# Summed weight blocks by copies and adding transfers in DRAM, and accumulator marks taken into z2, in an attention-and-gMLP kernel

## The chip, the cores and the metric

The kernel runs on one core of a Trainium2 chip. The metric is device time in microseconds (us) of one execution. Five engines matter: TensorE (PE in the rows, with its weight loads as PEld), VectorE (DVE), ScalarE (ACT), GpSimd (POOL) and SyncE (SP). Transfers are started by SyncE (queue q1), GpSimd (q0) and ScalarE (q10), and are carried by sixteen DMA engines.

## The reference, cut to what matters

One input of 2048 tokens and 512 columns is normalised and goes through two branches: a local attention (32 heads of 16, eight taps two tokens apart) and a gMLP whose gate mixes all tokens with a matrix `w_sp` of 2048 x 2048.

```python
# xn = layernorm(x); F = 1792, Fh = 896
z  = gelu(xn @ w_in)                       # S x 1792
z1 = z[:, :Fh]; z2 = layernorm(z[:, Fh:])
g  = w_sp @ z2 + b_sp[:, None]             # 2048 x 2048 by 2048 x 896
b  = (z1 * g) @ w_out
s  = attention(xn @ wqkv) @ wo             # 8 taps, dilation 2, softmax
out = x + s * silu(b)
```

## The kernel before, in words

**Products.** Every fp32 matrix product is made of three matmuls over a high and a low part: high by high, high by low, low by high. The helper `split` makes the high part on ScalarE (L195) and the low part on VectorE (L197). A weight block of the program thus appears as `wsp_5r` (as loaded), `wsp_5h` and `wsp_5l`. The matmuls of the gate are at L825; a 128x512 product is what most of them do. Where `split` writes the operand that TensorE holds fixed, the rows call the target `BIG`.

**Stages, by TensorE's time.** An opening to 66 us; the three attention projections; z1 from 158 to 218 us (seven blocks of columns by four chunks of tokens, gelu at L709); z2 from 218 to 295 us; the gate to 574 us; then the output projections of the two branches, to 691 us. Attention itself (L573 to L646 on VectorE, L633 on GpSimd) has no place of its own: it has a low priority and fills VectorE and GpSimd from the projections to beyond 600 us. Its 32 score products are in the list `sums_of`, numbered in program order.

**z2.** A z2 row i holds two tiles of 128 tokens, i and 8 + i; there are eight rows. Each tile is made in two halves, 512 and 384 columns wide, with twelve matmuls each, and gelu at L733. VectorE takes the statistics (L742, L743) and adds epsilon to the variance (L745, operand `mvz`); GpSimd takes the power -1/2 and one product (L746, L748); two rows later ScalarE normalises (L754), `split` writes the result into `BIG`, and four subtractions and additions (L767) make the combinations that go to DRAM as `t_d`.

**The gate** is `w_sp @ z2` by a scheme of seven block products in place of eight, for two halves a = 0, 1 of the output rows: m1a, m1b, m2a, m2b, m6a, m6b, m7, m4, m5, m3. m1a starts at 295 us, m1b (its second half of accumulators) at 317, m6a at 386. Each product accumulates in the PSUM banks `banks[a, f]`, f = 0 to 3, which ScalarE fills first with the bias (`seed`, L843). A seed's values are added to only if a matmul has opened the bank. For half a = 1 the function `second_seeds`, the third step of m1a, does that by four matmuls of 512 columns (L984), whose result the seed overwrites; for a = 0 the z2 stage has opened them.

**Weight sums.** m6, m7, m5 and m3 take sums of blocks of `w_sp`. For each half a and each i of eight (sixteen rows in all), from t0, t1 (upper blocks) and l0, l1 (lower blocks):

```
s3 = l1 + t1    s1 = t0 + t1    s0 = t0 + s3    s2 = l0 + s0
```

The 128x512 sums go to DRAM (`sums_d`) and are loaded again as `ws_0r` and so on when a product wants them (`summed`). Six rows (a = 1, i = 0 to 5) are added on GpSimd in the opening and the projections. Eight rows (a = 0) are added on VectorE during z1 (`first_sums`, L393), loaded by SyncE's queue and stored by GpSimd's, in eight buffers (`t4`) that z1 and z2 results, `z1_d` loads and others share. The last two (a = 1, i = 6, 7) are added on VectorE in the buffers of loaded weights (`raw_sums`) during z2.

**What sets the order.** Each engine runs its instructions in one fixed order. A planner with its own model of durations makes it, from priorities and from the dependencies, the ones added by hand among them (`add_manual_dep`). A dependency called NOSYNC binds the order on one engine and makes no wait of its own; SYNC makes the instruction wait. One by hand puts attention product `sums_of[9]` behind the low part of the first weights: `first weights ahead`.

## Time and profile before

| | |
|---|---|
| median of 3 runs | 695.89 us (694.54 to 697.04) |
| profiled execution: its own time | 696.54 us |
| its span (first to last instruction) | 694.8 us |
| busy: TensorE, VectorE, ScalarE, GpSimd | 686.6, 619.4, 277.7, 215.2 us |
| share of 16 DMA engines: q1, q0, q10 | 43.6%, 20.9%, 11.7% |
| DRAM read, written | 122.4 MB, 59.3 MB |
| granted TensorE clock | 1.00 in all stages |

How to read the rows that come later. A row of the timeline gives start, duration, engine, line, operation, what it writes and reads, the shapes, and in brackets how long the engine had stood before it and what released it. Starts of TensorE's rows are the firm part; durations of matmuls overlap, so two starts are subtracted to get the cost of one. A row of groups gives the busy time and the mean in ns of one, and behind the next bar the idle time ahead of such instructions and what ended it. A row of windows gives the stretch, its length, and for PE, PEld, DVE, ACT, POOL and SP the busy time with the number of instructions, then the clock, the DMA share and GB/s. TensorE is busy nearly all the time, so an instruction of another engine matters when TensorE stands for it, and else not.

### The profile page before, as it was taken

What the parts mean: (1) busy time and instruction counts of PE and PEld (TensorE: products, weight loads), DVE (VectorE), ACT (ScalarE), POOL (GpSimd) and SP (SyncE); (2) the same over time, 40 slices, a digit from 0 to 9 for tenths busy, and PEclk for the clock granted to TensorE, in tenths of its full rate; (3) what the DMA queues carried; (4) which work ended last, traced back from release to release, by engine and by line L of the source; (5) the groups of instructions that cost most, each with busy time, mean ns of one, the idle gap of its engine ahead of it and who ended that gap; (6) DMA issues with size and microseconds to landing.
All of it is one profiled execution on the core that took longest, in us unless ns stands there. A gap on an engine that the chain in (4) does not pass through costs nothing.

```text
span 694.8 us, 9233 instructions
## 1 busy us (share of the span) xinstructions
PE 686.6 (99%) x3084; PEld 573.0 (82%) x3084; DVE 619.4 (89%) x866; ACT 277.7 (40%) x458; POOL 215.2 (31%) x242
## 2 busy tenths in 40 slices
PE   8999999999999999998999999999999999999998
PEld 7888888888888899986888888888888888888886
DVE  6776868999989989889999998999989999989775
ACT  4342234224424256865534544442334444211531
POOL 3104837372343322124123222223111201642320
PEclk9999999999999999999999999999999999999999
DMA  8769899969999865267899768667576692655796
GB/s 270 252 193 289 288 348 384 346 204 358 407 412 340 329 231 190 80 201 231 258 403 314 284 211 298 208 232 248 183 261 206 215 342 89 221 173 190 246 330 235
DMA packets 102223, 182.36 MB, mean 262 GB/s; under 512 B 9184, under 2 KB 45280, under 8 KB 102176
## 3 DMA queue, kind: packets, MB, share of 16 engines
q1 hardware_dynamic: 56624, 102.21, 43.6%
q0 software_dynamic: 13824, 52.24, 20.9%
q10 hardware_dynamic: 31728, 27.33, 11.7%
q8 instruction: 24, 0.39, 0.2%
q14 instruction: 23, 0.19, 0.1%
HBM read 122.42 MB, written 59.32 MB: 262 GB/s over the span
## 4 chain that ended last, share of the span: by engine, by line
PE 67%; DVE 13%; DMA 12%; ACT 3%; issue 3%; POOL 1%; SPq 1%; DVEq 0%; POOLq 0%; ACTq 0%
PE g L825 35%; PE b L1067 4%; PE b L1069 4%; PE b L1068 4%; PE qkv L387 4%; PE qkv L386 4%; PE qkv L385 4%; DMA sb<-in_w_sp 3%; PE s L1069 2%; PE s L1068 2%; PE s L1067 2%; DMA sums_d<-sb 2%; DVE zst L742 2%; DMA z_d<-z1t 1%; DVE xT L280 1%
## 5 line engine op out<-in xcount | busy, mean ns | idle before, releaser
L633 POOL TENSOR_TENSOR pv<-pv 128x1024 f32<-128x1024 f32 x29 | 69.6, 2399 | 96.2 <-DVE pv L620 85.9
L573 DVE TENSOR_TENSOR pr<-k,q 128x2048 f32<-128x2048 f32 x32 | 73.6, 2299 | 2.0 <-DMA k<-qkv_d 1.9
L620 DVE TENSOR_TENSOR pv<-v,lg 128x2048 f32<-128x2048 f32 x32 | 74.6, 2331 | 0.7
L580 DVE TENSOR_REDUCE lg<-pr 128x128 f32<-128x2048 f32 x32 | 73.0, 2281 | 0.1
L647 POOL DMA_DIRECT2D o_d<-tt x32 | 18.0, 562 | 138.9 <-DVE tt L646 103.8
L433 ACT ACTIVATE stage<-qkv 128x512 f32<-128x512 f32 x40 | 23.0, 590 | 30.8 <-DMA qkv_d<-stage 17.0
L807 POOL DMA_DIRECT2D ol<-o_d x32 | 17.7, 555 | 37.7 <-DVE BIG L197 11.1
L1078 ACT ACTIVATE bt<-b 128x512 f32<-128x512 f32 x16 | 9.4, 599 | 43.5 <-PE b L1069 39.4
L709 ACT ACTIVATE z1t<-z 128x512 f32<-128x512 f32 x28 | 15.5, 597 | 26.1 <-DMA z_d<-z1t 15.3
L280 DVE TENSOR_TENSOR xT<-xT,mr 128x512 f32<-128x512 f32 x20 | 14.9, 743 | 11.9 <-DMA mr<-mv_d 6.4
L732 PE MATMUL z<-w_0h,BIG 128*128 128x512 f32 x64 | 25.0, 391 | 0.0
L731 PE MATMUL z<-w_0l,BIG 128*128 128x512 f32 x64 | 25.0, 391 | 0.0
L730 PE MATMUL z<-w_0h,BIG 128*128 128x512 f32 x64 | 24.9, 390 | 0.0
L742 DVE BATCH_NORM_STATS2 zst<-zt 128x6 f32<-128x448 f32 x32 | 19.3, 613 | 6.1 <-ACT zt L733 6.0
L754 ACT ACTIVATE zt<-zt,nmz,mvz 128x896 f32<-128x896 f32 x16 | 17.5, 1129 | 18.0 <-POOL nmz L748 18.0
L638 DVE TENSOR_TENSOR pv<-pv 128x512 f32<-128x512 f32 x32 | 22.9, 716 | 0.0
L733 ACT ACTIVATE zt<-z 128x512 f32<-128x512 f32 (+1 forms) x32 | 15.9, 536 | 15.2 <-DMA sums_d<-sa 14.0
L732 PE MATMUL z<-w_1h,BIG 128*128 128x384 f32 x64 | 21.5, 336 | 0.0
L730 PE MATMUL z<-w_1h,BIG 128*128 128x384 f32 x64 | 21.5, 335 | 0.0
L731 PE MATMUL z<-w_1l,BIG 128*128 128x384 f32 x64 | 21.4, 335 | 0.0
L393 POOL TENSOR_TENSOR sb<-sa,sb 128x512 f32<-128x512 f32 x12 | 19.7, 1644 | 5.4 <-DMA sb<-in_w_sp 5.1
L195 ACT ACTIVATE BIG<-zl 128x512 fp32r<-128x512 f32 x20 | 12.5, 630 | 21.6 <-DVE zl L895 19.8
(478 smaller groups left out, 2296.2 us busy)
## 6 DMA issues: line engine op xcount, KB each, us to landing
qkv_d<-stage ACTq DMA_DIRECT2D x24, 512.0 KB
v<-qkv_d POOLq DMA_DIRECT2D x14, 704.0 KB, 5.4
k<-qkv_d POOLq DMA_DIRECT2D x13, 704.0 KB, 6.8
sums_d<-sa POOLq DMA_DIRECT2D x14, 512.0 KB, 7.8
sums_d<-sb POOLq DMA_DIRECT2D x14, 512.0 KB, 8.0
z_d<-z1t ACTq DMA_DIRECT2D x14, 512.0 KB
zl<-z_d SPq DMA_DIRECT2D x12, 512.0 KB
tr<-t_d SPq DMA_DIRECT2D x12, 384.0 KB
```

Of the source, the lines that this page charges most:

```text
L573: line(nc.vector.tensor_tensor(pr, taps(ks[u], j0), qb.unsqueeze(1).to_broadcast([P, W, NJ * CS]), op=ALU.mult))
L580: line(nc.vector.tensor_reduce(lgs[u][:, j0 * HS : (j0 + NJ) * HS].rearrange("p i w -> p w i"), pr.rearrange("p w (i d) -> p w i d", d=DH) ...
L620: line(nc.vector.tensor_tensor(pv.rearrange("p w (i d) -> p w i d", d=DH), taps(vs[u], j0).rearrange("p w (i d) -> p w i d", d=DH), lgs[u] ...
L633: eng.tensor_tensor(pv[:, 0:4], pv[:, 0:4], pv[:, 4:8], op=ALU.add)
L730: nc.tensor.matmul(pz, xh[:, k], wh, start=k == 0, stop=False)
L731: nc.tensor.matmul(pz, xh[:, k], wl, start=False, stop=False)
L732: nc.tensor.matmul(pz, xl[:, k], wh, start=False, stop=k == KB - 1)
L742: nc.vector.bn_stats(st[:, h], zt[:, h * FQ : (h + 1) * FQ])
L825: nc.tensor.matmul(pg, z[a], w[b], start=start and i == 0, stop=stop and i == 2, skip_group_check=seeded)
L1067: nc.tensor.matmul(pp[:, cols], hi, wh, start=k == 0, stop=False)
L1068: nc.tensor.matmul(pp[:, cols], hi, wl, start=False, stop=False)
L1069: nc.tensor.matmul(pp[:, cols], lo, wh, start=False, stop=k == n - 1)
```

## The change

**Sums.** Ten of the sixteen rows (all eight of a = 0 and i = 6, 7 of a = 1) are no longer added by VectorE. They are taken in five pairs of neighbouring rows (`THEIRS`). For each pair ScalarE's queue copies l1, t0, t0 and l0 from `w_sp` to four DRAM tensors `sums_q` (twenty copies, 16 x 8192 elements each), and GpSimd's queue adds t1, s3, t1 and s0 onto them by transfers that accumulate at the destination (twenty, 256 x 512 each). They come in five rounds, in which a sum is used only a round after it was made. `go_on` paces them: fourteen operations in z1 (at every second gelu), sixteen in z2 (at the gelu of each narrow half), ten in the products m1b, m2a and m2b. A copy is paced by order (NOSYNC), an adding transfer waits for the ScalarE instruction that it is tied to (SYNC). The six rows on GpSimd stay.

**Marks.** The four matmuls of `second_seeds` go. In z2 rows 6 and 7 the first matmul of each narrow half is 512 wide in place of 384 (the first 128 columns repeat columns of the wide half), covers the whole bank, and so opens the banks that the second half's seeds are put in. The narrow halves' results now lie in the last 384 columns of the bank.

**A product waits.** The dependency of `sums_of[9]` goes; `sums_of[12]` is put behind the epsilon step of the last z2 row (L774 of the new file, L745 of the old).

```diff
+MINE = HT - 2
+THEIRS = [(0, q) for q in range(HT // 2)] + [(1, q) for q in range(MINE // 2, HT // 2)]
...
-    sums_d = dram.tile([2, 2, HT, P, 2, CT], F32, name="sums_d")
+    sums_d = dram.tile([2, MINE, P, 2, CT], F32, name="sums_d")
+    sums_q = {
+        (a, n, q): dram.tile([2, P, CT], F32, name=f"sums_{a}_{n}_{q}")
+        for a, q in THEIRS
+        for n in range(4)
+    }
...
-    def added(ts, eng):
-        t0, t1, l0, l1 = ts
-        for out_, p_, q_ in ((l1, t1, l1), (t1, t0, t1), (t0, t0, l1), (l0, t0, l0)):
-            eng.tensor_tensor(out_, p_, q_, op=ALU.add)
-
-    def block_sums(a, i, tile_=None, eng=nc.vector, loads=nc.sync, stores=nc.scalar, behind=None):
-        top, low = [(tile_ or t4)(f"s{n}_{a}_{i}") for n in "ab"]
-        for t, r in ((top, 0), (low, HT)):
-            ins = loads.dma_start(t, w_sp[2 * a : 2 * a + 2, r + i].rearrange("c p t -> p c t"))
-            if behind:
-                tc.add_manual_dep(ins.ins, behind[0].ins.name, behind[1], reason="sums later")
-        added([top[:, 0], top[:, 1], low[:, 0], low[:, 1]], eng)
-        for r, t in enumerate((top, low)):
-            stores.dma_start(sums_d[a, r, i], t)
-
-    def raw_sums(a, i):
-        ts = [
-            fetch(w_sp[2 * a + c, r + i], CT, f"sr_{a}_{i}_{c}_{r}") for r in (0, HT) for c in range(2)
-        ]
-        added(ts, nc.vector)
-        for n, t in enumerate(ts):
-            nc.sync.dma_start(sums_d[a, n // 2, i, :, n % 2], t)
...
-    z1_sums = [(0, i) for i in range(HT)]
+    def pool_sums(i, *behind):
+        top, low = [early_tile(f"s{n}_{i}") for n in "ab"]
+        for t, r in ((top, 0), (low, HT)):
+            ins = nc.gpsimd.dma_start(t, w_sp[2:4, r + i].rearrange("c p t -> p c t"))
+            tc.add_manual_dep(ins.ins, behind[0].ins.name, behind[1], reason="sums later")
+        t0, t1, l0, l1 = [top[:, 0], top[:, 1], low[:, 0], low[:, 1]]
+        for out_, p_, q_ in ((l1, t1, l1), (t1, t0, t1), (t0, t0, l1), (l0, t0, l0)):
+            nc.gpsimd.tensor_tensor(out_, p_, q_, op=ALU.add)
+        for r, t in enumerate((top, low)):
+            nc.gpsimd.dma_start(sums_d[r, i], t)
+
+    def rows_of_2k(blocks_):
+        return blocks_.rearrange("s p t -> (s p t)").rearrange("(r x) -> r x", x=4 * CT)
+
+    def raw_blocks(a, n, q):
+        r, c = divmod(n, 2)
+        j = r * HT + 2 * q
+        return w_sp[2 * a + c, j : j + 2]
+
+    def copied(to, a, q, src):
+        return nc.scalar.dma_start(rows_of_2k(sums_q[a, to, q]), rows_of_2k(src(a, q))), NOSYNC
+
+    def plus(to, a, q, src):
+        ins = nc.gpsimd.dma_start(
+            rows_of_2k(sums_q[a, to, q]), rows_of_2k(src(a, q)), accum_op=ALU.add, max_dma_last_dim=2048
+        )
+        return ins, SYNC
+
+    def weight_sums():
+        t0, t1, l0, l1 = [lambda a, q, n=n: raw_blocks(a, n, q) for n in range(4)]
+        s0, s3 = [lambda a, q, n=n: sums_q[a, n, q] for n in (0, 3)]
+        rounds = (
+            ((copied, 3, l1),),
+            ((copied, 0, t0), (plus, 3, t1)),
+            ((plus, 0, s3), (copied, 1, t0)),
+            ((plus, 1, t1), (copied, 2, l0)),
+            ((plus, 2, s0),),
+        )
+        for ops in rounds:
+            for a, q in THEIRS:
+                for fn, to, src in ops:
+                    yield fn, to, a, q, src
+
+    coming_sums = weight_sums()
+
+    def go_on(n, behind):
+        for fn, *args in itertools.islice(coming_sums, n):
+            ins, how = fn(*args)
+            tc.add_manual_dep(ins.ins, behind.ins.name, how, reason="sums paced")
...
-    def first_sums(a, i):
-        block_sums(a, i, stores=nc.gpsimd)
-
-    first_sums(*z1_sums[0])
-
     for f in range(FB):
         pair_ = side_pair("w1_last") if f == FB - 1 else None
         wh, wl = prep(w_in1[:, f, :], KB * P, f"w1_{f}", pair_=pair_)
@@ -706,31 +730,36 @@
             if c % 2 == 0:
                 zp = t4(f"z1t_{f}_{c}")
             zt = zp[:, c % 2]
-            nc.scalar.activation(zt, pz, AF.Gelu_apprx_tanh)
+            out_of = nc.scalar.activation(zt, pz, AF.Gelu_apprx_tanh)
             if c % 2:
+                go_on(1, out_of)
                 nc.scalar.dma_start(z1_d[f, c - 1 : c + 1].rearrange("c p t -> p c t"), zp)
-        if f == 2:
-            first_sums(*z1_sums[FB])
-        if f < FB - 1:
-            first_sums(*z1_sums[f + 1])
...
-        (k, h): prep(w_in2[:, k, HALF[h]], WID[h], f"w2_{k}_{h}")
+        (k, h): prep(
+            w_in2[:, k, slice(FH - CT, FH) if (k, h) == (0, 1) else HALF[h]],
+            CT if (k, h) == (0, 1) else WID[h],
+            f"w2_{k}_{h}",
+        )
         for h in range(2)
         for k in range(KB)
     }
 
     def z2_half(j, h, zt):
         xh, xl = xn_at(j)
-        pz = mm(f"z2_{j}_{h}")[:, : WID[h]]
+        bank = mm(f"z2_{j}_{h}")
+        pz = bank[:, CT - WID[h] :]
         for k in range(KB):
-            wh, wl = [w[:, : WID[h]] for w in w2[k, h]]
-            nc.tensor.matmul(pz, xh[:, k], wh, start=k == 0, stop=False)
+            wh, wl = [w[:, CT - WID[h] :] if k == 0 else w[:, : WID[h]] for w in w2[k, h]]
+            if k == 0 and j % HT >= HT - 2:
+                nc.tensor.matmul(bank, xh[:, k], w2[k, h][0], start=True, stop=False)
+            else:
+                nc.tensor.matmul(pz, xh[:, k], wh, start=k == 0, stop=False)
             nc.tensor.matmul(pz, xh[:, k], wl, start=False, stop=False)
             nc.tensor.matmul(pz, xl[:, k], wh, start=False, stop=k == KB - 1)
-        nc.scalar.activation(zt[:, HALF[h]], pz, AF.Gelu_apprx_tanh)
+        return nc.scalar.activation(zt[:, HALF[h]], pz, AF.Gelu_apprx_tanh)
...
-        nc.vector.tensor_scalar(rstd, rstd, EPS, None, op0=ALU.add)
+        known = nc.vector.tensor_scalar(rstd, rstd, EPS, None, op0=ALU.add)
+        if i == HT - 1:
+            tc.add_manual_dep(sums_of[12].ins, known.ins.name, NOSYNC, reason="gate rows ahead")
...
-        if i in (1, 3):
-            raw_sums(1, HT - 2 + i // 2)
         if i < HT:
             raw_z[i] = [t4(f"zt_{j}").rearrange("p i t -> p (i t)")[:, :FH] for j in (i, HT + i)]
             for h in range(2):
                 for j, zt in zip((i, HT + i), raw_z[i]):
-                    z2_half(j, h, zt)
+                    out_of = z2_half(j, h, zt)
+                    if h:
+                        go_on(1, out_of)
...
+            if name != "m1a":
+                go_on(1, highs[-1])
...
-            pair_ = spatial.get((2 * a + c, js)) or spatial_block(2 * a + c, js)
-            if (a, c, js) == (0, 0, 6):
-                tc.add_manual_dep(
-                    sums_of[9].ins, lows[-1].ins.name, NOSYNC, reason="first weights ahead"
-                )
-            return pair_
+            return spatial.get((2 * a + c, js)) or spatial_block(2 * a + c, js)
...
-        return lambda s: prep(sums_d[a, half_, s, :, i], CT, f"ws_{a}{half_}{i}_{s}")
+        def w(s):
+            if a and s < MINE:
+                src = sums_d[half_, s, :, i]
+            else:
+                src = sums_q[a, 2 * half_ + i, s // 2][s % 2]
+            return prep(src, CT, f"ws_{a}{half_}{i}_{s}")
+
+        return w
...
     def second_seeds():
-        for f in range(ODD + 1):
-
-            nc.tensor.matmul(
-                banks[1, f], z2_block(0, f)[0], half(0), start=True, stop=True
-            )
         for f in range(ODD + 1):
             seed(1, f, biases[1][0])
```

Lines of the new file are higher by some 30: `split` is at L202 and L204, the seeds at L874, the epsilon step at L774, the attention pair at L649 and L609, the gate products at L930, the copies at L420.

ScalarE's order at the seeds, first before, then with the change (`wsp_nh` are weights of m1a and, from 0 again, of m1b; `g_0` to `g_3` are the seeded banks; `zt` the last z2 row):

```order
L195 ACTIVATE wsp_1h<-wsp_1r 128x512
L195 ACTIVATE wsp_2h<-wsp_2r 128x512
L195 ACTIVATE wsp_3h<-wsp_3r 128x512
L195 ACTIVATE wsp_4h<-wsp_4r 128x512
L195 ACTIVATE wsp_5h<-wsp_5r 128x512
L843 ACTIVATE g_0_3191<-b_bh 128x512
L843 ACTIVATE g_1_3192<-b_bh 128x512
L843 ACTIVATE g_2_3195<-b_bh 128x512
L843 ACTIVATE g_3_3196<-b_bh 128x512
L754 ACTIVATE zt_3059<-zt_3059,nmz,mvz 128x896
```

```order
L202 ACTIVATE wsp_0h<-wsp_0r 128x512
L202 ACTIVATE wsp_1h<-wsp_1r 128x512
L420 DMA sums_2_2_92<-in_w_sp 16x8192
L874 ACTIVATE g_0_3129<-b_bh 128x512
L874 ACTIVATE g_1_3130<-b_bh 128x512
L874 ACTIVATE g_2_3133<-b_bh 128x512
L874 ACTIVATE g_3_3134<-b_bh 128x512
L785 ACTIVATE zt_2995<-zt_2995,nmz,mvz 128x896
L785 ACTIVATE zt_2996<-zt_2996,nmz,mvz 128x896
L202 ACTIVATE wsp_2h<-wsp_2r 128x512
```

The seeds stood behind the high parts of wsp_1 to wsp_5; they stand behind wsp_1 now, with a copy ahead of them.

VectorE's order around the last z2 row's epsilon step (`mvz` of L745, now L774), first before, then with the change:

```order
L197 TENSOR_TENSOR wsp_0l<-wsp_0r,wsp_0h 128x512
L197 TENSOR_TENSOR wsp_1l<-wsp_1r,wsp_1h 128x512
L1006 TENSOR_TENSOR b_bl<-b_bh,b_bl 128x512
L573 TENSOR_TENSOR pr_4_1457<-k_0_1440,q_0_1441 128x2048
L638 TENSOR_TENSOR pv_4_1452<-pv_4_1452 128x512
L767 TENSOR_TENSOR zt_2975<-zt_2975 128x384
L743 BN_AGGR mvz<-zst_3153 128x2
L197 TENSOR_TENSOR wsp_2l<-wsp_2r,wsp_2h 128x512
L197 TENSOR_TENSOR wsp_3l<-wsp_3r,wsp_3h 128x512
L639 TENSOR_TENSOR pv_4_1452<-pv_4_1452 128x4x2x32
L767 TENSOR_TENSOR zt_2975<-zt_2975,zt_2976 128x384
L745 TENSOR_SCALAR mvz<-mvz 128x2
```

```order
L204 TENSOR_TENSOR BIG<-zt_2909,BIG 128x4x128
L204 TENSOR_TENSOR wsp_7l<-wsp_7r,wsp_7h 128x512
L771 BN_STATS zst_3091<-zt_2996 128x6
L798 TENSOR_TENSOR zt_2909<-zt_2909 128x384
L204 TENSOR_TENSOR BIG<-zt_2910,BIG 128x7x128
L772 BN_AGGR mvz<-zst_3091 128x2
L204 TENSOR_TENSOR wsp_0l<-wsp_0r,wsp_0h 128x512
L798 TENSOR_TENSOR zt_2909<-zt_2909,zt_2910 128x384
L204 TENSOR_TENSOR wsp_1l<-wsp_1r,wsp_1h 128x512
L774 TENSOR_SCALAR mvz<-mvz 128x2
L649 TENSOR_TENSOR pv_0_1531<-v_0_1525,lg_1464 128x2048
L609 TENSOR_REDUCE lg_1505<-pr_4_1518 128x8x16
```

The epsilon step stood behind the splits of wsp_0 to wsp_3 and two attention steps. With the change no attention step is left between the split of wsp_6 and it, and the product of 2048 columns (`pv`, L649) follows it.

VectorE's order at the start of m6a (`ws` are its summed weights, `zl` the gate products that wait for m2b's accumulators, `tr` the loaded combinations), first before, then with the change:

```order
L895 TENSOR_TENSOR zl_0_3829<-g_0_3191,zl_0_3829 128x512
L614 TENSOR_TENSOR lg_1485<-lg_1485,sm_1547 128x256
L197 TENSOR_TENSOR BIG<-tr_2_3907,BIG 128x2x3x128
L197 TENSOR_TENSOR ws_4l<-ws_4r,ws_4h 128x512
L620 TENSOR_TENSOR pv_0_1551<-v_1_1545,lg_1485 128x2048
L580 TENSOR_REDUCE lg_1525<-pr_4_1538 128x8x16
L895 TENSOR_TENSOR zl_0_3829<-g_1_3192,zl_0_3829 128x512
L895 TENSOR_TENSOR zl_2_3836<-g_2_3195,zl_2_3836 128x512
L197 TENSOR_TENSOR ws_5l<-ws_5r,ws_5h 128x512
L895 TENSOR_TENSOR zl_2_3836<-g_3_3196,zl_2_3836 128x512
L197 TENSOR_TENSOR BIG<-tr_4_3944,BIG 128x2x3x128
L197 TENSOR_TENSOR ws_6l<-ws_6r,ws_6h 128x512
```

```order
L930 TENSOR_TENSOR zl_2_3780<-g_3_3134,zl_2_3780 128x512
L204 TENSOR_TENSOR ws_2l<-ws_2r,ws_2h 128x512
L675 STREAM_TRANSPOSE tt_0_1631<-pv_0_1612 128x256
L204 TENSOR_TENSOR ws_3l<-ws_3r,ws_3h 128x512
L204 TENSOR_TENSOR BIG<-tr_0_3817,BIG 128x2x3x128
L649 TENSOR_TENSOR pv_4_1634<-v_0_1606,lg_1545 128x2048
L609 TENSOR_REDUCE lg_1626<-pr_0_1627 128x8x16
L204 TENSOR_TENSOR BIG<-tr_2_3851,BIG 128x2x3x128
L204 TENSOR_TENSOR ws_4l<-ws_4r,ws_4h 128x512
L204 TENSOR_TENSOR ws_5l<-ws_5r,ws_5h 128x512
L204 TENSOR_TENSOR ws_6l<-ws_6r,ws_6h 128x512
```

Before, the split of ws_4 and an attention pair (L620, L580) stood ahead of the last three gate products. Now all four are ahead of the splits of ws_2 to ws_4, and the attention pair stands between ws_3 and ws_4.

6 lines of the change are left out of this document (2 added, 4 removed).

## The prediction

> **What bounds the kernel now.** I read the page first (busy time and the chain), then TensorE's waits, then the timeline around the longest of them.
>
> ```profile
> span 694.8 us, 9233 instructions
> PE 686.6 (99%) x3084; PEld 573.0 (82%) x3084; DVE 619.4 (89%) x866; ACT 277.7 (40%) x458; POOL 215.2 (31%) x242
> PE 67%; DVE 13%; DMA 12%; ACT 3%; issue 3%; POOL 1%; SPq 1%; DVEq 0%; POOLq 0%; ACTq 0%
> ```
>
> TensorE is busy 99% of the span, but the chain runs over VectorE and DMA for a quarter of it: a busy TensorE was kept company by a second chain about as long. The waits say how often that second chain won.
>
> ```profile
> PE g L825 <- ACT g L843: 1.9, 1, 1.9
> PE g L825 <- ACT BIG L195: 0.2, 1, 0.2
> ```
>
> Everything else that TensorE waited for lies in the opening or is 0.2 us. So the change can act on TensorE's own work and on these two waits, and on nothing else but waits that it makes. The timeline prices them:
>
> ```profile
> 311.26 0.39 PE L825 MATMUL g<-wsp_5h,BIG 128*128 128x512 f32 x1
> 311.49 1.07 PE L984 MATMUL g<-BIG 128*128 128x512 f32 x4
> 312.39 0.39 PE L825 MATMUL g<-wsp_6h,BIG 128*128 128x512 f32 x1
> ...
> 314.89 0.39 PE L825 MATMUL g<-wsp_6h,BIG 128*128 128x512 f32 x1
> 317.17 0.50 PE L825 MATMUL g<-wsp_0h,BIG 128*128 128x512 f32 x1 [1.90 <-ACT g L843]
> 317.51 0.40 PE L825 MATMUL g<-wsp_0l,BIG 128*128 128x512 f32 x1
> ...
> 323.88 0.39 PE L825 MATMUL g<-wsp_3h,BIG 128*128 128x512 f32 x1
> 324.48 0.50 PE L825 MATMUL g<-wsp_7h,BIG 128*128 128x512 f32 x1 [0.21 <-ACT BIG L195]
> 324.81 0.39 PE L825 MATMUL g<-wsp_7l,BIG 128*128 128x512 f32 x1
> ```
>
> Durations overlap, so I count from start to start: a 512-wide matmul costs 0.227 us (311.26 to 311.49). The four marking matmuls cost 312.39 - 311.49 = 0.90. The first wait costs 2.28 instead of 0.23, and the matmul behind it 0.34: 2.16 lost. The second costs 0.60 and 0.33: 0.47 lost. All that there is to gain is 0.90 + 2.16 + 0.47 = 3.5 us, 0.5% of the span.
>
> **Why TensorE waited there.** The rows of the other engines, ScalarE first, then VectorE:
>
> ```profile
> 236.39 0.98 ACT L733 ACTIVATE zt<-z 128x512 f32<-128x512 f32 x2 [13.09 <-DMA sums_d<-sa]
> ...
> 313.99 0.64 ACT L195 ACTIVATE wsp_3h<-wsp_3r 128x512 fp32r<-128x512 f32 x1 [5.03 <-DMA wsp_3r<-in_w_sp]
> 315.37 0.63 ACT L195 ACTIVATE wsp_4h<-wsp_4r 128x512 fp32r<-128x512 f32 x1 [0.75 <-PE g L825]
> 316.53 2.14 ACT L843 ACTIVATE g<-b_bh 128x512 f32<-128x512 f32 x4
> ```
>
> ```profile
> 304.04 2.29 DVE L620 TENSOR_TENSOR pv<-v,lg 128x2048 f32<-128x2048 f32 x1
> 306.24 2.28 DVE L580 TENSOR_REDUCE lg<-pr 128x128 f32<-128x2048 f32 x1
> ...
> 318.58 0.16 DVE L745 TENSOR_SCALAR mvz<-mvz 128x2 f32<-128x2 f32 x1
> ```
>
> The four seeds of the second half (L843) stand on ScalarE behind weight copies that waited for a load, and for TensorE itself. Behind that is lateness from further back: the first z2 row's gelu stood 13.09 us for a buffer whose stores of summed weights had not landed, and at 304 VectorE put 4.4 us of attention ahead of the last z2 row, whose statistics were done only at 318.58.
>
> **The change, part by part.**
>
> *Marks and widening.* The marks go: -0.90. Four opening matmuls grow from 384 to 512 columns:
>
> ```profile
> L730 PE MATMUL z<-w_0h,BIG 128*128 128x512 f32 x64 | 24.9, 390 | 0.0
> L730 PE MATMUL z<-w_1h,BIG 128*128 128x384 f32 x64 | 21.5, 335 | 0.0
> ```
>
> 4 x (390 - 335) ns = +0.22. Both lie on TensorE with nothing beside them: -0.68, the sure part.
>
> *The first wait.* With no mark to wait for, the seeds need a free bank and the bias, and the new order has them behind wsp_1h and ahead of wsp_2h, so neither the load of 313.99 nor TensorE stands before them. They can run at about 309 to 311, and TensorE comes to them at about 314.4. Bounds 0 and -2.16; I take all of it, since both things that ended last there are behind the seeds now.
>
> *The gate on the last row (sums_of[12]).* The new VectorE order has, between the split of wsp_6 (done 304.04, by the start of the next row) and the row's mvz, ten operations: four of 512 (0.60 each by the m6 rows below), one of 896 (1.0), two of 384 (0.46), and the statistics (0.7): 5.0 us, so mvz at 309.1 instead of 318.58. GpSimd's power and products come next:
>
> ```profile
> 318.82 1.68 POOL L746 TENSOR_TENSOR mvz<-mvz,nhalf 128x2 f32<-128x2 f32 x1 [1.83 <-DVE mvz L745]
> 320.60 1.50 POOL L748 TENSOR_SCALAR nmz<-mvz 128x1 f32<-128x1 f32 x2
> ```
>
> GpSimd takes 1.8 to 3.2 us for these, ScalarE 2.1 for the two normalisations, 1.0 for wsp_2h and wsp_3h, 0.5 for the copy into BIG: row 7 arrives at 314.5 to 315.9. The new order wants it two matmuls into the second half, at 314.9: a wait of 0 to 1.0, in place of 0.47. Bounds -0.47 and +0.5; I take -0.2, because the lateness behind 304 shrinks too (next). Queued behind the gate on VectorE are the attention steps from pv(12) on; GpSimd's folds and the o_d stores wait for them, TensorE does not before 650 us, and it shows no wait there now.
>
> *The sums leave VectorE.*
>
> ```profile
> L393 DVE TENSOR_TENSOR sb<-sa,sb 128x512 f32<-128x512 f32 x16 | 11.3, 714 | 2.2 <-DMA sb<-in_w_sp 2.1
> L393 DVE TENSOR_TENSOR sa<-sa 128x512 f32<-128x512 f32 x8 | 5.4, 682 | 0.1
> L393 DVE TENSOR_TENSOR sa<-sa,sb 128x512 f32<-128x512 f32 x8 | 5.4, 681 | 0.1
> ```
>
> These 32 adds (22.1 us) and eight on raw tiles go, and with them the buffers that the 13.09 us stood on. Attention fills the time; TensorE waits for neither, so by itself I cost this at nothing. What it buys is z2 rows on time, the cover for the last two terms.
>
> *The transfers.*
>
> ```profile
> q1 hardware_dynamic: 56624, 102.21, 43.6%
> q0 software_dynamic: 13824, 52.24, 20.9%
> sums_d<-sb POOLq DMA_DIRECT2D x14, 512.0 KB, 8.0
> ```
>
> By these rows 512 KB (0.524 MB) take 0.524/52.24 x 20.9% x 694.8 = 1.46 us of all sixteen engines on GpSimd's queue and 1.55 on SP's; I use 1.5. Removed are 40 such transfers' worth (ten rows, four each): 60 us. Added are 20 copies (30 us) and 20 adds. No adding transfer is in the trace: one pass each is the lower bound (30 us), three (source, old value, result) the upper (90 us). I take two, 60 us: nearer the plain store than the upper end, since the old value is the only extra read. Net +30 us of engine time, spread thus:
>
> ```profile
> 158.00:228.00 70.00, 70.00 (x316) 58.69 (x315) 67.30 (x85) 25.81 (x42) 26.55 (x32) 1.00 1.01 381
> 228.00:262.00 34.00, 34.00 (x168) 30.11 (x167) 30.63 (x55) 15.33 (x26) 7.68 (x12) 1.00 0.69 263
> 262.00:306.00 44.00, 44.00 (x217) 39.15 (x216) 37.31 (x77) 32.55 (x52) 8.83 (x15) 1.00 0.47 154
> 328.00:392.00 64.00, 64.00 (x284) 52.99 (x283) 62.50 (x84) 28.05 (x47) 16.55 (x17) 1.00 0.89 313
> ```
>
> (The last three columns are clock, DMA share and GB/s.) The removed 60 us lie in the first two rows, so the full stretch to 228 empties; about six adds and four copies come into 262 to 306, which is half idle. Seven adds and three copies come into 328 to 392, where 7 us are free: that is the risk, priced as a rival. Issuing is covered: 20 copies at about 0.4 us on ScalarE, less than half busy up to 262, and 20 adds on GpSimd, where 16 stores of about the same price go. An add also waits for a ScalarE result and for the round before it; queued behind it on GpSimd are folds, attention loads and the z2 powers. The rounds are tens of us apart against 8.0 to land, so I cost that at nothing.
>
> The Trainium skill, "DMA: Bandwidth & Descriptors", section "Issuing engines are not separate DMA queues", says that transfers started by any engine run on the same sixteen engines; its section "Rules for kernel authors" says that an accumulating transfer reads its destination and writes it later. The share of 1.01 with three queues in use agrees with the first; no run here shows the second yet. They speak for the third rival.
>
> *The start of m6a.* In the new order VectorE splits ws_2 to ws_7 behind the last of the four gate products that wait for m2b's end (before, ws_4 was still ahead of three of them).
>
> ```profile
> 385.81 0.39 PE L825 MATMUL g<-ws_0h,BIG 128*128 128x512 f32 x1
> ```
>
> ```profile
> 385.85 0.68 DVE L197 TENSOR_TENSOR ws_4l<-ws_4r,ws_4h 128x512 fp32r<-128x512 f32 x1
> 386.45 2.28 DVE L620 TENSOR_TENSOR pv<-v,lg 128x2048 f32<-128x2048 f32 x1
> 388.66 2.28 DVE L580 TENSOR_REDUCE lg<-pr 128x128 f32<-128x2048 f32 x1
> 390.85 1.28 DVE L895 TENSOR_TENSOR zl<-g,zl 128x512 f32<-128x512 f32 x2
> ```
>
> Counted from m6a's first matmul, the last product can start at about 0.3. Then come product, ws_2, transpose, ws_3, an operand of 768 columns, an attention pair, another operand and ws_4: 5 x 0.6 less one still to come, 0.36, 2 x 0.87, 2 x 2.2, and ws_4's own 0.67, so 9.2 to 9.3. TensorE wants it after 39 matmuls, at 8.84: a wait of about 0.5. If VectorE is as late as in the rows above, where products that could start near 386.1 started at 390.85, it is 0.5 + 4.7 = 5.2. I take 0.5: with the gate at 309.1, the shapes of the rows up to there add up to 377.5, before the bank is done, so VectorE should wait for TensorE there.
>
> **The sum**, on the profiled execution's 696.54: -0.68 - 2.16 - 0.2 + 0.5 = -2.5, so 694.0. That execution lies 0.65 above the median of the runs shown (695.89); against the median the same sum gives **693.3 us**, 0.37% faster.
>
> **Rivals.**
> 1. *The waits move, they do not go* (row 7 or m6a takes about 2 us): -0.68 and little else, 695.2. For it: 62.5 of 64 us of VectorE are busy in 328 to 392, so any slip is passed on. Against: 27 us of its work are gone. 0.32.
> 2. *VectorE is late at m6a as before*: 695.89 - 0.68 - 2.36 + 5.2 = 698.1, slower. It decides from a lateness of about 2.6 us on, where 0.5 + 2.6 eats the 3.0 gained. 0.10.
> 3. *The adds fill the engines in 328 to 392.* At two passes, 7 x 3.0 + 3 x 1.5 = 25.5 us against 7 free; 18 us too much. Attention's transfers can give way, weight loads cannot for long; if a third reaches TensorE, 693.3 + 6 = about 699; at three passes 36 against 7, and past 702. At one pass it is nothing. 0.12.
>
> My forecast has 0.46. About 0.3% (2.1 us, near the spread of the runs shown) is what can be told from no change: faster is the forecast (0.46), same the first rival (0.32), slower the other two (0.22). The range runs from 692.2 (all 3.5 gained, less the widening, and a little noise) to 698.5 (takes in rivals 1 and 2 and the near edge of 3); the forecast's own is 692.3 to 693.8.
>
> **What would show it.** Right: no PE wait on the seeds (L874 now), ScalarE's first z2 gelu without a wait for sums, mvz of the last row before 311, a wait of under 1 us at m6a's ws_4l, and a share below 1 in 158 to 228. Wrong: a PE wait of over 1.5 us on BIG or ws_4l; a share above 0.95 in 328 to 392 with waits for wsp loads; adds landing in over 16 us; or folds on GpSimd waiting behind an add.

## The result, and the profile after

| | before | with the change |
|---|---|---|
| median | 695.38 us (694.54 to 697.04, 4 runs) | 740.04 us (738.02 to 741.58, 4 runs) |
| ratio | | 1.0637, 95% interval 1.0598 to 1.0677 |
| profiled execution, own time and span | 696.54, 694.8 us | 741.58, 739.8 us |
| mean granted TensorE clock | 1.000 | 0.972 |

The change makes the kernel 6.4% slower; the forecast was 0.37% faster (693.3 us, range 692.2 to 698.5). First the page of the changed kernel, its span and busy times:

```profile
span 739.8 us, 9132 instructions
PE 697.3 (94%) x3080; PEld 579.6 (78%) x3080; DVE 600.9 (81%) x826; ACT 283.5 (38%) x462; POOL 226.0 (31%) x246
```

The span grew by 45.0 us. TensorE has four matmuls fewer and is busy 10.7 us longer, at a granted clock below 1. Its waits (engine, line, what it waited for, total, times, longest), of which before had 1.9 and 0.2 us:

```profile
PE g L856 <- DVE wsp_12l L204: 13.5, 1, 13.5
PE g L856 <- ACT wsp_1h L202: 5.6, 1, 5.6
PE z L760 <- DVE lg L627: 4.7, 1, 4.7
PE g L856 <- ACT BIG L202: 4.5, 1, 4.5
PE g L856 <- ACT g L874: 2.8, 1, 2.8
PE g L856 <- DVE ws_4l L204: 2.6, 1, 2.6
```

TensorE's timeline at the longest one (start, duration, row), and the window around it, whose third number from the end is the clock:

```profile
400.00 0.39 PE L856 MATMUL g<-wsp_12h,BIG 128*128 128x512 f32 x1
413.86 0.79 PE L856 MATMUL g<-wsp_12l,BIG 128*128 128x512 f32 x1 [13.46 <-DVE wsp_12l L204]
414.45 0.63 PE L856 MATMUL g<-wsp_12h,BIG 128*128 128x512 f32 x1
414.87 0.63 PE L856 MATMUL g<-wsp_13h,BIG 128*128 128x512 f32 x1
415.30 0.63 PE L856 MATMUL g<-wsp_13l,BIG 128*128 128x512 f32 x1
...
392.00:425.00 33.00, 19.54 (x79) 15.62 (x78) 14.31 (x22) 4.11 (x8) 11.64 (x12) 0.79 0.78 206
```

Two costs stand here. One is the wait. The other comes behind it: from start to start the matmuls now take 0.42 to 0.43 us in place of 0.227, for some 4 us. Counted over the whole trace from 30 us on, the steps from start to start that are over 0.6 us too long are too long by 38.9 us together (nine of them; before, one of 2.1), and 55 steps that are less too long, by 10.4 us (before 1.1). Nearly all of the 55 lie in stretches where the trace's clock records stand at 0.50. Together that is 46.1 us more than before, against 45.0 us of span and 0.7 us of matmul work that the change takes away. So the loss is waits, and a slow clock behind the long ones. The Trainium skill, "TensorE: Matmul & The Clock Gate", section "Part 1: The HAM clock gate (the "warmup" mystery)", says that the array runs at half its clock until it has been busy for some 3.4 us; the trace agrees with half the clock and some 4 us of it, and the forecast had no such term.

Why VectorE brought wsp_12l so late. VectorE's timeline, then GpSimd's over the same time:

```profile
388.80 2.28 DVE L602 TENSOR_TENSOR pr<-k,q 128x2048 f32<-128x2048 f32 x1
410.38 0.69 DVE L667 TENSOR_TENSOR pv<-pv 128x512 f32<-128x512 f32 x1 [19.30 <-POOL pv L662]
...
413.12 0.68 DVE L204 TENSOR_TENSOR wsp_12l<-wsp_12r,wsp_12h 128x512 fp32r<-128x512 f32 x1
```

```profile
376.12 0.95 POOL L423 DMA_DIRECT2D sums<-sums  x1 [3.88 <-ACT BIG L202]
385.19 0.89 POOL L423 DMA_DIRECT2D sums<-sums  x1 [8.11 <-issue]
394.83 0.88 POOL L423 DMA_DIRECT2D sums<-sums  x1 [8.74 <-issue]
400.60 0.89 POOL L423 DMA_DIRECT2D sums<-sums  x1 [4.89 <-issue]
406.49 0.88 POOL L423 DMA_DIRECT2D sums<-sums  x1 [5.00 <-issue]
...
407.67 2.67 POOL L662 TENSOR_TENSOR pv<-pv 128x1024 f32<-128x1024 f32 x1
```

The five adding transfers of the last round stand in a row on GpSimd, and attention's fold (L662) behind them. VectorE stood 19.3 us for that fold, with the weight split behind it in its own order. The view of these transfers gives their time to landing:

```profile
DMA to landing us min/median/max: 5.4/5.6/9.3
```

The starts are 9.07, 9.64, 5.77 and 5.89 us apart: each starts when the one before has landed, in this trace 0.32 to 0.34 us behind it. "issue" means that the profile shows nothing else that it waited for; the ScalarE results that they are tied to were ready by 381.6 (ScalarE's timeline), and none of them waits for the semaphore of the one ahead.

The seeds did not come at 309 to 311. They waited for the bias, whose load SyncE issued only at 323.35 (ScalarE's row, SyncE's row):

```profile
334.62 2.16 ACT L874 ACTIVATE g<-b_bh 128x512 f32<-128x512 f32 x4 [10.55 <-DMA b_bh<-in_b_sp]
...
323.35 0.42 SPq L1014 DMA_DIRECT2D b_bh<-in_b_sp  x1
```

One name in the text ahead needs a correction: the list `sums_of` holds attention's products with v, not its scores, so `sums_of[12]` is the `pv` of L649 that follows the epsilon step in the order shown.

### The profile page after: what moved, and what is told of

Its sections match the earlier page's. It is cut to its first block, busy times and chain, and to the rows that moved or that the text cites. A ratio compares the mean times of both kernels' runs of the same rounds, so it can differ in the third digit from the quotient of the medians.

```text
span 739.8 us, 9132 instructions
## 1 busy us (share of the span) xinstructions
PE 697.3 (94%) x3080; PEld 579.6 (78%) x3080; DVE 600.9 (81%) x826; ACT 283.5 (38%) x462; POOL 226.0 (31%) x246
## 4 chain that ended last, share of the span: by engine, by line
PE 55%; DVE 16%; DMA 12%; issue 10%; ACT 4%; POOL 2%; ACTq 0%; DVEq 0%; POOLq 0%; SPq 0%
PE g L856 26%; DMA v<-qkv_d 4%; PE b L1098 3%; PE b L1099 3%; PE b L1097 3%; DVE lg L609 3%; DMA qkv_d<-stage 3%; DVE pv L649 2%; PE qkv L392 2%; DVE pr L602 2%; PE qkv L393 2%; PE qkv L394 2%; PE s L1099 2%; PE s L1098 2%; PE s L1097 2%
## 5 line engine op out<-in xcount | busy, mean ns | idle before, releaser
L662 POOL TENSOR_TENSOR pv<-pv 128x1024 f32<-128x1024 f32 x29 | 70.1, 2418 | 87.4 <-DVE pv L649 75.5
L649 DVE TENSOR_TENSOR pv<-v,lg 128x2048 f32<-128x2048 f32 x32 | 74.5, 2330 | 10.9 <-DMA v<-qkv_d 10.3
L602 DVE TENSOR_TENSOR pr<-k,q 128x2048 f32<-128x2048 f32 x32 | 73.2, 2289 | 5.7 <-DMA k<-qkv_d 4.9
L609 DVE TENSOR_REDUCE lg<-pr 128x128 f32<-128x2048 f32 x32 | 73.0, 2281 | 0.1
L667 DVE TENSOR_TENSOR pv<-pv 128x512 f32<-128x512 f32 x32 | 22.9, 716 | 19.4 <-POOL pv L662 19.3
L635 ACT ACTIVATE lg<-lg 128x256 f32<-128x256 f32 x16 | 6.6, 411 | 60.1 <-DVE lg L630 60.1
L1158 DVE TENSOR_TENSOR sg<-s,sg 128x512 f32<-128x512 f32 (+2 forms) x17 | 11.2, 659 | 15.5 <-PE s L1099 15.4
L287 DVE TENSOR_TENSOR xT<-xT,mr 128x512 f32<-128x512 f32 x20 | 13.7, 687 | 11.3 <-DMA mr<-mv_d 6.5
L423 POOL DMA_DIRECT2D sums<-sums x10 | 9.2, 923 | 44.2 <-issue 26.7
L856 PE MATMUL g<-ws_5h,BIG 128*128 128x512 f32 x52 | 20.7, 402 | 0.0
```

The costliest lines, as they stand in the source:

```text
L602: line(nc.vector.tensor_tensor(pr, taps(ks[u], j0), qb.unsqueeze(1).to_broadcast([P, W, NJ * CS]), op=ALU.mult))
L609: line(nc.vector.tensor_reduce(lgs[u][:, j0 * HS : (j0 + NJ) * HS].rearrange("p i w -> p w i"), pr.rearrange("p w (i d) -> p w i d", d=DH) ...
L649: line(nc.vector.tensor_tensor(pv.rearrange("p w (i d) -> p w i d", d=DH), taps(vs[u], j0).rearrange("p w (i d) -> p w i d", d=DH), lgs[u] ...
L662: eng.tensor_tensor(pv[:, 0:4], pv[:, 0:4], pv[:, 4:8], op=ALU.add)
L856: nc.tensor.matmul(pg, z[a], w[b], start=start and i == 0, stop=stop and i == 2, skip_group_check=seeded)
```

## The experiments

Theories at the start. **A**: GpSimd is held by the adding transfers, and what stands behind them (folds, attention loads) makes VectorE late. **B**: the copies and adds fill the DMA engines. **C**: the new order is at fault, whatever the transfers do. Later ones are named where they come up. All times below are medians; the kernel before ran 694.0 to 695.8 us beside them.

| run | sums of the ten rows | gate | us | ratio to before (95%) |
|---|---|---|---|---|
| no sums | left out | 9 | 692.70 | 0.9963 (0.9951 to 0.9975) |
| copies only | left out, 20 copies | 9 | 695.80 | 1.0004 (0.9981 to 1.0027) |
| plain, old gate | left out, 40 plain transfers | 9 | 703.34 | 1.0140 (1.0122 to 1.0159) |
| all apart, behind | 20 copies, 20 adds | 9 | 710.43 | 1.0202 (1.0177 to 1.0228) |
| all apart | the same | 9 | 716.46 | 1.0311 (1.0284 to 1.0339) |
| last five apart | the same | 9 | 716.53 | 1.0321 (1.0294 to 1.0349) |
| old gate | as in the change | 9 | 728.40 | 1.0486 (1.0445 to 1.0527) |
| no sums, new gate | left out | 12 | 700.78 | 1.0090 (1.0066 to 1.0114) |
| plain | left out, 40 plain transfers | 12 | 715.82 | 1.0294 (1.0265 to 1.0322) |
| last five apart | 20 copies, 20 adds | 12 | 726.26 | 1.0457 (1.0434 to 1.0479) |
| the change | 20 copies, 20 adds | 12 | 740.04 | 1.0637 (1.0598 to 1.0677) |

("Gate 9" is the dependency of before, "gate 12" that of the change; the marks are gone in all of these.)

### The parts alone

The marks alone (before, with the diff's z2 and `second_seeds` parts):

> The kernel before with only the four marking matmuls gone and the four narrow halves opened 512 wide; sums and gate as before. Theories A and B: nothing of the loss is here; -0.68 on TensorE's own work and up to -2.2 of the seeds' wait, so 692.5 to 695. Theory C: the seeds now stand early on ScalarE behind a late bias load, 700 or more.

Measured: 696.1 us (12 runs, 692.6 to 697.7), ratio 1.0002 (0.9984 to 1.0021). No change that can be told, and 1.1 us above the most that A and B expected; C falls for this part. Its profiled execution (693.79) has no wait for the seeds left, and they waited 0.16 us for the bias there, so the forecast's wait does go in such an execution, but the runs spread as before.

The marks and the moved gate, with the sums still on VectorE:

> As the run with only the marks, and the gate moved: attention product 12 behind the last z2 row's epsilon step in place of product 9 behind the first weights. Theories A and B: 692 to 696. Theory C (gate and order): 710 or more.

Measured: 711.89 us, ratio 1.0239 (1.0214 to 1.0264). So the gate costs 16 us by itself here, as C said. But VectorE still makes the sums in this kernel, so it does not yet price the gate in the change.

The sums alone (the change, with marks, narrow halves and gate put back):

> The changed kernel with the marks, the narrow halves and the gate put back as before, so that only the sums by copies and adding transfers are new. Theories A and B: nearly all of the loss is here, 725 to 750. Theory C: 695 to 705.

Measured: 739.6 us, ratio 1.0640 (1.0601 to 1.0680). The sums alone give the whole loss, A or B; the longest wait is 18.0 us, again on a weight (wsp_13l) behind an 18.0 us wait of VectorE for a fold. The parts do not simply add, though: the same sums and gate with the four marks gone (728.40 us, "old gate" in the table) is 11.2 us faster, while the marks alone changed nothing. TensorE's waits of 0.9 us and more behind the opening add up to 33.1 us here, 3.2 of them for the seeds, and to 26.1 there, with 0.3 for the seeds; the orders differ, too, and the rest of it stays open.

### Adding against plain transfers, and the gate

```diff
-            ..., accum_op=ALU.add, max_dma_last_dim=2048
+            ..., max_dma_last_dim=2048
```

> The changed kernel with its twenty adding transfers as plain copies of the same size on the same queue, in an order of instructions that is the same on all engines. The sums are left out by it (the last source stands where the sum should), so the output is another. Theory A (GpSimd is held: an adding transfer starts only 0.33 us after the one before it landed, and folds and attention loads stand behind it): VectorE's wait of 19.3 us for the fold falls below 2, the five last transfers start under 1 us apart, TensorE's wait of 13.5 us on wsp_12l goes, and the time is 700 to 715. Theory B (the copies and adds fill the DMA engines): the copies still run, one read of three less per add, so 730 or more. Theory C (the new order is at fault, whatever the transfers do): 735 or more.

Measured: 715.82 us. The order is the same on all engines and the bytes written are the same, so 24 of the 45 us are what adding costs over copying. GpSimd's timeline at the last round, now:

```profile
363.59 0.58 POOL L423 DMA_DIRECT2D sums<-sums  x1 [4.61 <-ACT BIG L202]
364.58 0.58 POOL L423 DMA_DIRECT2D sums<-sums  x1 [0.41 <-ACT wsp_9h L202]
365.36 0.56 POOL L423 DMA_DIRECT2D sums<-sums  x1 [0.20 <-issue]
370.28 0.56 POOL L423 DMA_DIRECT2D sums<-sums  x1 [4.36 <-ACT lg L635]
372.21 0.56 POOL L423 DMA_DIRECT2D sums<-sums  x1 [1.38 <-issue]
...
373.36 2.41 POOL L662 TENSOR_TENSOR pv<-pv 128x1024 f32<-128x1024 f32 x1
```

They take 8.6 us together in place of 30.4, and the fold is not late. The 20 us that are left over are not this hold.

```diff
-            tc.add_manual_dep(sums_of[12].ins, known.ins.name, NOSYNC, ...)
+            # and in plain(), at block (0, 0, 6), as before:
+                tc.add_manual_dep(sums_of[9].ins, lows[-1].ins.name, NOSYNC, ...)
```

With plain transfers, and then with the adding ones:

> The changed kernel with plain copies in place of the adding transfers (so the sums are left out, as in the first run) and with the gate put back: attention product 9 behind the first weights, none behind the last z2 row. Theory A with G (the gate lets three more attention products into z2, some 9 us of VectorE each, while z2's rows need VectorE, and that is the rest of the loss): 696 to 704, z2's second row known at about 250 in place of 267 to 273, no wait of TensorE above 3 us. Rival B (transfers fill the DMA engines in z1 and z2, so VectorE stands for v loads): about 712 to 716, as with the moved gate.

> The changed kernel with only the gate put back; adding transfers as in the change. Theory A: the five last adding transfers still stand in a row on GpSimd ahead of a fold, so a wait of TensorE of over 10 us in the second block products and 725 to 742, though the gate's part (about 16 us, if G holds) is gone: the held queue costs more where attention is behind. Rival G alone (the gate is all of it): 700 to 725.

Measured: 703.34 and 728.40 us. The gate's price is 12.5 us with plain transfers and 11.6 with adding ones; the adding's is 24.2 with the gate of the change and 25.1 with the old one. The two add up and do not hang on each other. G (named in the first of the two expectations) holds but for one sign, a wait of 3.8 us where none above 3 was expected; A holds for the adding; "the gate is all of it" falls by a little (728.4 against at most 725).

Is the gate's price its own? Neither copies nor adding transfers, and the plain upper blocks loaded where a sum should be, with the old gate and with the new:

```diff
-                src = sums_q[a, 2 * half_ + i, s // 2][s % 2]
+                src = raw_blocks(a, i, s // 2)[s % 2]
-        for fn, *args in itertools.islice(coming_sums, n):
+        for fn, *args in ():
```

> The changed kernel with the gate put back and neither copies nor adding transfers for the ten rows: the plain upper blocks of the weights are loaded where a sum should be, so this part of the sums is left out. It shows what the change could have brought at best. If the copies and adds cost only by holding queues and DMA engines: 692 to 696. If the order that the planner made without VectorE's sums is itself worse: 698 to 703. In z1 VectorE should still stand for attention loads, since its freed 22 us cannot be used by a chain of fold, load and product: idle of 8 us or more between 158 and 228.

> The changed kernel, gate as in the change, with neither copies nor adding transfers (sums left out as in the run before). If the gate costs by itself, by three more attention products among the z2 rows: 700 to 706, z2's second row known later than 262 and TensorE waiting for wsp_1 at m1a's start. If it cost only because the transfers had made attention late: 692 to 696.

Measured: 692.70 us and 700.78 us, so the gate costs 8.1 us with none of the forty transfers. The windows of attention's score products (L602) over z2, 218 to 295 us, in the first and the second kernel (busy time, and in brackets how many), and the second kernel's waits on TensorE:

```profile
218.00:295.00 77.00, 0.75 (x1) 1.00 0.22 75
```

```profile
218.00:295.00 77.00, 9.31 (x4) 1.00 0.32 111
```

```profile
PE g L856 <- ACT wsp_1h L202: 2.7, 1, 2.7
PE g L856 <- DVE wsp_1l L204: 2.4, 1, 2.4
```

The gate is not only a wait for product 12; it also lets products 9 to 11 go ahead, which the old one held until m1a. In z2 they take VectorE from the statistics and splits: the second row's epsilon step came at 261.8 us in place of 238.9, and TensorE stood for the first weights of m1a (at 304 in the change: 5.6 and 1.5 us).

The run with no sums shows a guess of mine to be wrong, too: VectorE's idle time between 158 and 228 us was 6.3 us, not 8 or more. In the change it is 11.2 us, because attention's loads are late there.

### Apart: the last five, then all twenty

The last round's transfers each behind a fold of their own (`folds` lists the instructions of L662):

```diff
+    for n in (15, 17, 19, 21, 23):
+        go_on(1, folds[n])        # by order only, in place of m2a and m2b
```

> The changed kernel with the last round's five adding transfers each behind a fold of its own (every second one from fold 15 on), so that none follows another before it has landed; the same bytes are moved and added. Theory A: the wait of 19.3 us of VectorE for a fold and TensorE's 13.5 us go, with the slow matmuls behind it: 712 to 724. Theory B (bytes): 733 or more, since all bytes are still moved.

> Both: the last five adding transfers apart, and the gate put back. A with G: 697 to 708, near the run with plain copies and the gate put back. If the fifteen adding transfers in z1 and z2 hold GpSimd enough by themselves: 710 to 725. Theory B: 725 or more.

Measured: 726.26 and 716.53 us: 13.8 and 11.9 us less than with the five in a row, and VectorE's wait of 19.3 us is gone. A is right on that place, though the first came 2 us above its range. The same bytes are moved, so B does not explain this part. The second came in its second case: some 13 us remain above plain transfers with the old gate, and the fifteen transfers before have to account for them.

All twenty apart, each behind a fold or a z2 product on GpSimd, old gate:

> The gate put back, and all twenty adding transfers apart, each behind a fold or a z2 product on GpSimd (by order only, no wait for ScalarE), so that none comes within a landing time of another; the same bytes. Theory A (only the holding costs): 699 to 707, near the 703.3 of plain copies with the gate put back. If an adding transfer also costs by its bytes or by slowing others' loads: 708 to 716, near the 716.5 of the run with only the last five apart. Nothing starts 0.33 us behind another's landing.

Measured: 716.46 us. None follows another's landing any more, and yet nothing is won: A falls for the first fifteen. Between the opening and 500 us TensorE has one long wait left, in z2's first row, and the slow clock behind it. The wait, GpSimd's rows in z1, and the time to landing of the load in the second of them:

```profile
PE z L756 <- DVE lg L621: 14.5, 1, 14.5
```

```profile
190.36 0.91 POOL L423 DMA_DIRECT2D sums<-in_w_sp  x1
190.96 0.91 POOL L585 DMA_DIRECT2D v<-qkv_d  x1
...
DMA to landing us min/median/max: 13.2/13.2/13.2
```

The load of v, issued 0.6 us behind an adding transfer, landed 13.2 us later, 2.5 us behind that transfer (190.36 + 11.3 = 201.6); the next such load took 13.8. VectorE stood 8.4 and 9.1 us for them, with a z2 weight split (w_1l) behind. That is theory **Q**: GpSimd's queue delivers in order. The test moves z1's adding transfers away from these loads:

> As the run with all twenty adding transfers apart, but with none right ahead of an attention load of v while z1 runs: the ones of z1 stand behind folds 4, 6 and 8, whose next load is a product later, the rest behind z2's products and later folds. Theory Q (GpSimd's queue delivers in order, so a load issued behind an adding transfer lands behind it): v loads in z1 land in 7 to 10 us in place of 13.2 and 13.8, the 14.7 us of TensorE at 224 fall to under 4, and the time is 698 to 706. Rival (the adding transfers slow all loads by their bytes): v loads still over 11 us, 710 to 717.

Measured: 710.43 us, 6 us less; the loads of v in z1 land in 9.5 to 10.2 us, the wait at 224 is 6.2 us. The loads agree with Q but for 0.2 us, and the rival's are over 11 us; the time and the wait missed Q's ranges, and the time lies in the rival's. The traces show the order itself: in all eighteen no transfer of GpSimd's queue landed ahead of one issued before it. So Q is right in kind, and not the whole: 10.2 us with no adding transfer right ahead is more than the 5.1 to 5.9 us without sums. So the copies alone:

> The changed kernel with the gate put back, the twenty copies as in the change, and no adding transfers; the plain upper blocks are loaded where a sum should be, so the sums are left out. If the copies on ScalarE's queue slow the attention loads in z1: v loads there land in 7.5 us or more, VectorE stands for them, and the time is 697 to 703, most of what plain transfers cost. If they don't: v loads in 5 to 6.5 us and 692 to 695, as with no sums.

Measured: 695.80 us, in a wide spread of 692.75 to 699.43, and loads of v in z1 in 7.8 to 9.5 us. The mechanism is as expected (the copies slow these loads, VectorE stands 9.9 us for them), its price of 3.1 us over no sums is less than the 4 or more expected, and it varies from run to run. With all twenty apart and behind the loads, 7.1 us more than with plain transfers and the old gate (703.34) remain; TensorE's one long wait there is the 6.2 us at 224.

### Why an adding transfer is held

Two theories were left. **O**: adding transfers are kept in order, one at a time. **R**: there is room in GpSimd's queue for so many rows, and one transfer of 256 rows of 2 KB nearly fills it.

```diff
-            ..., accum_op=ALU.add, max_dma_last_dim=2048
+            ..., accum_op=ALU.add, max_dma_last_dim=8192
```

> The changed kernel, its adding transfers in 64 rows of 8 KB in place of 256 of 2 KB; the order of VectorE, ScalarE, TensorE and SyncE is the same, bytes too. Theory R (room in GpSimd's queue, counted in rows): no hold, the five last start as soon as ScalarE's weights allow, under 2 us apart, TensorE's 13.5 us on wsp_12l go, and the time is 712 to 722, near the 715.8 of plain copies. Theory O (adding transfers are kept in order): each still starts 0.33 us after the landing before it, 732 to 745.

```diff
+            for r in (slice(0, 32), slice(32, 64)):
+                nc.gpsimd.dma_start(rows_of_2k(...)[r], rows_of_2k(...)[r], accum_op=ALU.add, ...)
```

> The changed kernel, each adding transfer as two of 128 rows of 2 KB, one right behind the other. Theory R: the two halves start together, and the first half of the next one waits until a half before it has landed; the whole holds for about as long as before, 732 to 748. Theory O: the second half starts only when the first has landed, so forty landings in place of twenty, 745 or more, with 0.3 us between each landing and the next start.

Measured: 729.87 and 726.14 us. GpSimd's rows at the last round, first with rows of 8 KB, then with halves:

```profile
370.84 0.84 POOL L423 DMA_DIRECT2D sums<-sums  x1 [3.32 <-ACT BIG L202]
371.89 2.42 POOL L423 DMA_DIRECT2D sums<-sums  x3 [0.21 <-issue]
379.47 0.77 POOL L423 DMA_DIRECT2D sums<-sums  x1 [5.17 <-ACT lg L635]
```

```profile
369.58 2.62 POOL L424 DMA_DIRECT2D sums<-sums  x3 [3.26 <-ACT BIG L202]
377.39 0.82 POOL L424 DMA_DIRECT2D sums<-sums  x1 [5.18 <-issue]
379.26 0.81 POOL L424 DMA_DIRECT2D sums<-sums  x1 [1.06 <-issue]
381.31 0.84 POOL L424 DMA_DIRECT2D sums<-sums  x1 [1.23 <-issue]
...
DMA to landing us min/median/max: 7.5/8.8/10.3
```

O falls twice. With 64 rows each, four start within 2.5 us, long before any has landed. With 128 rows each, three start at once; the fourth, fifth and sixth each start 0.30 to 0.31 us after the first, second and third have landed (at 377.08, 378.96 and 381.00 in the trace). So three times 128 adding rows are out at a time and four are not, and of 256 rows only one. R is what the starts show. Plain transfers take room, too, but less: of 256 rows three went out within 1.8 us (above), and the fourth and fifth started 0.33 and 0.31 us after the first and second had landed. Counted over all eighteen traces, with an adding row as two, GpSimd's queue never has more than 896 rows out, and some hundred issues that would have made it 1024 or more start 0.26 to 0.39 us behind the landing that made room. A row of 8 KB counts no more than one of 2 KB, so it is rows and not bytes; that an adding row takes the room of two is read off the traces and not explained. The kernel before shows the limit as well, at its fourth plain load of 256 rows in a row (the first landed at 61.99):

```profile
62.31 0.73 POOL L398 DMA_DIRECT2D sb<-in_w_sp  x1 [5.02 <-issue]
```

The times were not as R expected, though: without the hold 729.87 us, not 712 to 722, and with halves 726.14, not 732 to 748. What took the hold's place is B, in this stretch. The window of the kernel with 8 KB rows, and a wait of its ScalarE:

```profile
350.00:392.00 42.00, 42.00 (x187) 34.75 (x187) 32.71 (x41) 11.45 (x19) 13.46 (x15) 1.00 0.99 301
```

```profile
ACT wsp_12h L202 <- DMA wsp_12r<-in_w_sp: 8.9, 1, 8.9
```

All sixteen engines are full, and ScalarE waits 8.9 us for a weight load; TensorE stands 4.9 us for it. The stretch is as full in the change (1.01) and with plain transfers (1.02), but this load, issued at 375.00, let ScalarE start only at 397.75, after 22.7 us; with plain transfers it was 12.0 (366.95 to 378.96). What an adding transfer costs the engines is in the queue rows of the change and of the kernel with plain transfers (packets, MB, share of 16 engines):

```profile
q0 software_dynamic: 16960, 54.34, 26.0%
```

```profile
q0 software_dynamic: 14400, 54.34, 21.5%
```

26.0% of 739.8 less 21.5% of 714.5 is 38.7 us, or 1.9 us for each of twenty transfers on top of a plain one.

### A version that is faster than both

Before, with the marks gone and only the last two rows of sums (a = 1, i = 6 and 7, on VectorE in z2 before) by four copies and four adding transfers, far apart and none ahead of a load of v; z1's sums and the gate as before:

```diff
-        if i in (1, 3):
-            raw_sums(1, HT - 2 + i // 2)
+        # four copies at the narrow halves of tiles 0 to 3; the adding transfers behind
+        # GpSimd's products of z2 rows 4 and 6 and behind folds 12 and 14
```

> The kernel before with the marks gone and only the last two rows of sums (a = 1, i = 6 and 7, on VectorE in z2 before) by four copies and four adding transfers, far apart and none ahead of a load of v; the gate as before and z1's sums still on VectorE. If the change's idea pays where the transfers hold nothing: 692.5 to 695, at most 0.4% faster than before. If any adding transfer on GpSimd's queue costs TensorE: 696 to 702.

Measured: 692.57 us (7 runs, 692.2 to 694.6), ratio 0.9962 (0.9945 to 0.9978). So 0.4% can be had where the transfers hold nothing; whether it comes from the adds that VectorE is spared or from the new order alone was not tried. TensorE's longest wait behind the opening, in the profiled execution:

```profile
PE b L1091 <- ACT wout_4h L196: 0.9, 1, 0.9
```

## Why the prediction was wrong, step by step

- **What bounds the kernel, and what there is to gain**: right. With no sums to make, TensorE has no wait left behind the opening and the time is 692.70 us, 0.6 below the forecast. The forecast is nearly the time of a kernel whose sums cost nothing.
- **The transfers, "costed at nothing"**: this is the step that failed. It said that the rounds are tens of us apart against 8.0 to land. That is true of one pair's rounds, but the five transfers of a round come one behind the other on GpSimd, and its fixed order has the last five in a row ahead of a fold; I named what is queued behind them and did not put the two together. It also took issuing as covered, at the price of a store: four of the last five issues stood 26.7 us on GpSimd until the one before had landed, and the kernel before had shown such a stand of 5.02 us at 62.31. Of the forecast's own signs of being wrong, the last one came true: folds on GpSimd waited behind an add. On top of no sums, with the old gate, the runs showed +3.1 us for the copies, +7.5 for plain transfers in place of the adds, and +25.1 for adding: of the last, 11.9 us go when the last five are set apart, and 18.0 when all are and z1's stand behind the loads.
- **The engine time of an adding transfer**: right in size. Two passes, 3.0 us, were taken; the queue rows show a plain transfer's 1.5 (the forecast's own row) plus 1.9, so 3.4.
- **The gate, -0.2 with bounds of half a us**: wrong in kind. The step counted what stands between wsp_6 and the last row's epsilon step, and found it short; it did not ask what the old dependency had kept out of z2. The epsilon step came at 326.1, not 309.1, and even with none of the transfers the gate did not bring it forward (313.0 us with it, 312.0 with the old one). The runs showed +8.1 to +12.5 us with VectorE's sums gone.
- **The sums leave VectorE, "attention fills the time"**: half right. It filled little of it in z1: 11.2 of 70 us stood idle, since the next product needs a load that lands 8.4 to 9.4 us after its issue; before, 2.7 us did, with loads in 7.1 to 8.3 us and sums to make meanwhile. The statement that TensorE waits for no attention step holds of the data, not of VectorE's order, where weight splits stand behind such steps. The waits of 13.5 us here, 18.0 with the sums alone and 14.5 with all twenty apart went this way.
- **The first wait, -2.16**: the mark is gone, but the seeds stood for the bias load, which the step named and did not look up. It was issued at 305.00 before, with the seeds at 316.53, and at 323.35 with the change, where TensorE stood 2.8 us for the seeds in place of 1.9.
- **m6a, +0.5**: 2.6 us on ws_4l, between the 0.5 taken and the 5.2 of the late case.
- **The rivals**: the third came nearest. Its place was right and its price of two passes nearly so, and with rows of 8 KB it appears as described, with a weight load late at full engines. But it was given 0.12 and priced at 699 to 702, and it lacked the hold, the gate and the slow clock behind the long stalls, which is a fifth of the loss by itself (9.3 of 45.0 us).

## What to carry to other kernels

Before work is moved to a queue, look at what stands behind it on that queue and on its engine, and at how many of its transfers are out at once; an engine in order passes one late load or fold on to everything behind it, weight splits for TensorE included. A dependency that is taken away lets something in: ask what it kept out of the stage. And price a stall of TensorE of a few us with the slow matmuls behind it (here some 1.4 to 3 us for one).
